# Fused RWKV attention and two MoE stages: filler transposes only in the first part, later expected landings, and a small expert slot whose first products keep the tokens stationary

## The chip, the cores and the metric

One core of a Trainium2 chip (trn2) runs the whole program in one launch. The metric is the device time of a run in microseconds (us); smaller is better. The engines are TensorE (PE; its weight loads are shown as PEld), VectorE (DVE), ScalarE (ACT), GpSimd (POOL) and SyncE (SP, which issues most DMAs). "PEq", "SPq" and so on are the engines' sequencers.

## What is computed

Three stages follow each other; 3072 tokens (4 sequences of 768), width 384.

```python
# 1. attention, 8 heads of 48, state S per head, in time order
y[t] = r[t] @ (S + outer(u * k[t], v[t]));  S = w * S + outer(k[t], v[t])
# 2. dense feed-forward layer, 384 -> 2048 -> 384
h = x @ w_in;  x2 = silu(h) @ w_out
# 3. top-1 mixture of 8 experts, 384 -> 1024 -> 384
logits = x2 @ w_gate + modality_bias[modality_id];  e = argmax(logits)
out = softmax(logits)[e] * (relu(x2 @ w1[e]) @ w2[e])
```

## The kernel before, in words

**Tiles.** Attention runs in chunks: 24 tiles of 128 tokens, tile n belonging to block j = n//3 of 384 tokens. `load_A` (L284, 768 KB, tile name in_av) and `load_B` (L287, 384 KB, in_rk) bring a tile's inputs into one of the buffers AB_132, AB_133 or `stall`. L460 (DVE) scales a tile by the decay table Pt, L464, L435 and L436 (POOL) do more of the scaling, L439 and L440 (DVE) a row sum, L487 and L503 (PE) are the products, L493 (DVE) masks them, L544 is the state's product. After the loads stands L425, a store that is taken only in a rare case, but whose place on SP waits for the landing of `load_A`.

**Dense layer.** `moe1` takes a block of 384 tokens through 16 chunks of the hidden width. Every 32-bit product is done as three products of high and low halves (hi by hi, hi by lo, lo by hi). L618 is a first product (9 matmuls, stationary 128x128, 384 columns moving), L622 and L623 the SiLU on ACT, L625 the low half on DVE, L637 the second products. L653 and L655 drain a block's result into x2all.

**Routing.** `route` transposes the block (L686, nine transposes), takes logits (L697) and a string of small DVE operations (L702 to L774), stores the tokens and their gate (`x_rows`, L764, three stores of 192.5 KB on SP) and scatters their numbers into the experts' lists (L780, POOL).

**Experts.** `expert(s)` is called for nine static slots, s = 0 to 8. Slots 0 to 7 hold 384 tokens each. Slot 8 is `small`: one tile of 128 tokens. First products are L949 (`e_g1`), relu and split are L1034 (ACT) and L1036 (DVE), second products L957 (`e_g2`), scaling by the gate L961 or L963, and the rows go out by an indirect DMA on POOL (L966). In the small slot there are two groups k of four chunks of the hidden width each: w1 stands as the stationary 128x128 operand and the 128 tokens move, so a group is 4 x 9 = 36 matmuls of 128 columns, and writes h transposed, as the second products need it. After the slots comes a loop for left-over tiles (L1077, L1078), which with these inputs runs no turn; the engines' sequencers meet at it.

**Order.** All of this up to the loop is not written in the order in which it runs. Every step is added to a `Plan` (class at L60, `add` at L65) with an engine, a duration, a priority, dependencies and buffers. `order()` (L74) plays it through when the program is built: a free engine takes the ready step with the lowest priority number; a DMA's data counts as landed 4.0 us after its share of one common transfer line. The steps are then issued sorted by planned start, so each engine has a fixed order and real waits are by semaphores. One hundred filler steps of four transposes of the identity each (L372, PE, priority 900 and up, called dummies below) take what PE time is left free in the plan.

Of the kernel before, what the change touches and what calls it, by code (L numbers as in the profile page):

```python
# [8 lines left out]
F32 = mybir.dt.float32  # L9
# [4 lines left out]
AF = mybir.ActivationFunctionType  # L14
ALU = mybir.AluOpType
AX = mybir.AxisListType
SP = mybir.EngineType.SP
# [9 lines left out]
KT = DM // 128  # L27
# [15 lines left out]
NZ = 9  # L43
# [13 lines left out]
class Plan:  # L57
# [7 lines left out]
    def add(self, eng, dur, prio, fn, deps=(), acq=(), rel=(), lat=0.2, nbytes=0):  # L65
        o = Op()
        o.eng, o.dur, o.prio, o.fn, o.lat, o.nbytes = eng, dur, prio, fn, lat, nbytes
        o.deps = [d for d in deps if d is not None]
        o.acq, o.rel = list(acq), list(rel)
        o.n, o.after, o.left = len(self.ops), [], 0  # L70
        self.ops.append(o)
        return o

    def order(self):  # L74
        for o in self.ops:
            o.left = len(o.deps)
            for d in o.deps:
                d.after.append(o)
        ready = {e: [] for e in ENGINES}
        busy = dict.fromkeys(ENGINES, 0.0)  # L80
        events, dma, t, done = [], 0.0, 0.0, []
        for o in self.ops:
            if not o.left:
                heapq.heappush(ready[o.eng], (o.prio, o.n, o))
        count = 0
        while True:
            moved = True
            while moved:
                moved = False
                for e in ENGINES:  # L90
                    if busy[e] > t + 1e-9 or not ready[e]:
                        continue
                    held, pick = [], None
                    while ready[e]:
                        x = heapq.heappop(ready[e])
                        need = {}
                        for p, _ in x[2].acq:
                            need[p] = need.get(p, 0) + 1
                        if all(len(self.free[p]) >= k for p, k in need.items()):
                            pick = x[2]  # L100
                            break
                        held.append(x)
                    for x in held:
                        heapq.heappush(ready[e], x)
                    if pick is None:
                        continue
                    o = pick
                    for p, key in o.acq:
                        self.slot[key] = (p, self.free[p].pop(0))
                    o.start = t  # L110
                    busy[e] = t + o.dur
                    end = t + o.dur + o.lat
                    if o.nbytes:
                        dma = max(dma, t + o.dur) + o.nbytes / 260e3
                        end = dma + 4.0
                    heapq.heappush(events, (busy[e], count, None))
                    heapq.heappush(events, (end, count + 1, o))
                    count += 2
                    done.append(o)
                    moved = True  # L120
            if not events:
                break
            t = events[0][0]
            while events and events[0][0] <= t + 1e-9:
                o = heapq.heappop(events)[2]
                if o is None:
                    continue
                for key in o.rel:
                    p, i = self.slot[key]
                    self.free[p].append(i)  # L130
                for a in o.after:
                    a.left -= 1
                    if not a.left:
                        heapq.heappush(ready[a.eng], (a.prio, a.n, a))
        assert len(done) == len(self.ops), (len(done), len(self.ops))
        self.span = t
        return sorted(done, key=lambda o: (o.start, o.n))


def moe_rwkv_kernel(tc, ins, out):  # L140
    nc = tc.nc
    vv, gp, act, pe, sp = nc.vector, nc.gpsimd, nc.scalar, nc.tensor, nc.sync
# [13 lines left out]
    hps = [ps.tile([128, 512], F32, name=f"ph{i}") for i in range(2)]  # L156
    aps = [ps.tile([128, 512], F32, name=f"pa{i}") for i in range(3)]
    tps = [ps.tile([128, 512], F32, name=f"pt{i}") for i in range(3)]
# [3 lines left out]
    ident = cst.tile([128, 128], F32, name="ident")  # L162
# [120 lines left out]
    def load_A(n, s):  # L283
        sp.dma_start(AB[s][:, 0:AW], ins["av"][n])  # L284

    def load_B(n, s, w_=0):
        sp.dma_start(AB[s][:, AW + w_ * DM:], ins["rk"][n * C:(n + 1) * C, w_ * DM:])  # L287
# [52 lines left out]
    for i in range(NP):  # L340
        n = 1 << i
# [12 lines left out]
    add = P.add  # L354
# [4 lines left out]
    def sl_(key):  # L359
        return P.slot[key][1]  # L360
# [47 lines left out]
    def attention(n):  # L408
# [5 lines left out]
        if n < 3:  # L414
            P.slot[kA] = ("tA", n)
            if n < 2:
                P.free["tA"].remove(n)
            oA, oB = gate((0.1, 0.2, 2.2)[n]), add("SP", 0.5, -49 + n, lambda: load_B(n, n, 1), nbytes=200e3)
        else:
            oA = add("SP", 0.6, z - 9, lambda: load_A(n, sl_(kA)), acq=[("tA", kA)], nbytes=786e3)  # L420
            oB = add("SP", 0.6, z - 8.9, lambda: load_B(n, sl_(kA), int(n < NZ)), [oA], nbytes=393e3 if n >= NZ else 197e3)
        relA = [kA] if n != 2 else []

        def f_V():
# [469 lines left out]
    def e_view(buf, p):  # L894
        t = W[p][buf].rearrange("p a b -> p (a b)")
        n = KT * FE
        return t[:, 0:n].rearrange("p (k f) -> p k f", k=KT), t[:, n:2 * n].rearrange("p (f d) -> p f d", f=NFE)
# [46 lines left out]
    def e_g1(buf, xb, fcs, n, p):  # L944
        w1h, w1l = e_view(buf, 0)[0], e_view(buf, 1)[0]
        for i, fc in enumerate(fcs):
            ops = [(kt, a, b_) for a, b_ in ((w1h, xh), (w1l, xh), (w1h, xl)) for kt in range(KT)]
            for m, (kt, a, b_) in enumerate(ops):
                pe.matmul(p[:, i * n:(i + 1) * n], a[:, kt, fc * 128:(fc + 1) * 128], b_[xb][:, kt, 0:n],  # L949
                          start=m == 0, stop=m == len(ops) - 1)  # L950

    def e_g2(buf, fcs, t, n, hi, lo, a):
        w2h, w2l = e_view(buf, 0)[1], e_view(buf, 1)[1]
        for i, fc in enumerate(fcs):
            sl = slice(i * n + t * 128, i * n + (t + 1) * 128)
            for m, (g, wt_) in enumerate(((hi, w2h), (hi, w2l), (lo, w2h))):
                pe.matmul(a[:, 0:DM], g[:, sl], wt_[:, fc, :], start=fc == 0 and m == 0, stop=fc == NFE - 1 and m == 2)  # L957
# [17 lines left out]
    def swap():  # L975
        at.release()
        ew = pools["ew"] = tc.alloc_tile_pool(name="ew", bufs=1)
        pools["raw"] = [ew.tile([128, KT * FE], F32, name=f"raw{i}") for i in range(4)]
        pools["xg"] = [ew.tile([128, XW], F32, name=f"xgb{i}") for i in range(2 * BT)]
        pools["gt"] = [[ew.tile([128, 1], F32, name=f"gt{i}{k}") for k in range(BT)] for i in range(NSTAT + 1)]  # L980

# [2 lines left out]
    def expert(s):  # L984
# [43 lines left out]
        for k, fcs in enumerate(groups):  # L1028
            kH, kG = ("eh", s, k), ("eg", s, k)
            m = n * step  # L1030
            o1 = add("PE", 2.7 if small else 1.57, z + k * (1.0 if small else 1.0), lambda fcs=fcs, kH=kH: e_g1(buf, xb, fcs, n, hps[sl_(kH)]),
                     [o_sp[0, p_] for p_ in range(3)] + o_x, acq=[("h", kH)])
            em["g1", s] = em["g1", s] + [o1]
            o2 = add("ACT", 0.62 if small else 0.5, z + k - 6, lambda kH=kH, kG=kG, m=m: act.activation(  # L1034
                ghb[sl_(kG)][:, 0:m], hps[sl_(kH)][:, 0:m], AF.Relu), [o1], acq=[("g", kG)])
            o3 = add("DVE", 0.7 if small else 0.57, z + k - 6, lambda kH=kH, kG=kG, m=m: vv.scalar_tensor_tensor(  # L1036
                glb[sl_(kG)][:, 0:m], hps[sl_(kH)][:, 0:m], 0.0, ghb[sl_(kG)][:, 0:m].bitcast(F32), op0=ALU.max, op1=ALU.subtract),
                [o2], rel=[kH])
            need = [o_sp[1, p_] for p_ in range(((0, 0, 0, 1, 1, 1, 2, 2)[fcs[-1]]) + 1)] + [o3, lastg]

            def f_g2(fcs=fcs, kG=kG):
                for t in range(nt_):
                    e_g2(buf, fcs, t, n, ghb[sl_(kG)], glb[sl_(kG)], aps[sl_(ka[t])])
            lastg = add("PE", 2.1 if small else 1.57, z + k + 2.3, f_g2, need, acq=[("a", q) for q in ka] if k == 0 else [], rel=[kG])
            em["g2", s] = em["g2", s] + [lastg]
# [27 lines left out]
        expert(s)  # L1073
    with tc.manual_schedule():
        for o in P.order():
            o.fn()
    tn = nc.values_load(tailn, min_val=0, max_val=NMAX - NSTAT + NA + 1)  # L1077
    with tc.For_i(0, tn, 1) as i:  # L1078
        e_ids("t", lists[1], bass.ds(i + (NSTAT - 1 - NA), 1))
# [91 lines left out]
```

## Time and profile before

| | us |
|---|---|
| median of three runs (lowest to highest) | 808.32 (807.42 to 811.14) |
| the profiled execution, its own time | 806.15 |
| its span in the trace | 804.4 |
| PE busy | 791.2 (98%) |
| DVE, ACT, POOL busy | 425.7, 337.3, 227.9 |
| mean granted TensorE clock | 0.995 |

The span runs from the first to the last instruction in the trace; the 1.75 us between it and the execution's own time lie outside. A busy share tells how full an engine is, not whether its work is of use: the dummies count as busy PE. The granted clock is the share of full TensorE speed that the chip allowed in a stretch; its two levels are 1.2 and 2.4 GHz, so 0.5 is the lower one.

### The profile page before, as it was taken

How to read it: one execution, taken by the hardware profiler on the slowest of the kernel's cores; microseconds unless marked ns; L12 is line 12 of the kernel's file. 1: busy time of each engine (PE TensorE's matmuls, PEld its weight loads, DVE VectorE, ACT ScalarE, POOL GpSimd, SP SyncE). 2: the span in 40 equal slices, each digit the busy share in tenths (PEclk: the TensorE clock that was granted, in tenths of full speed). 3: DMA queues.
4: the chain of work that ended last, by engine and by line, in shares of the span. 5: the costliest groups of instructions: out<-in, count | busy, mean ns of one | idle time of the engine just before them, and what ended most of it. 6: DMA issues, size and time to landing. Idle time of an engine off the chain costs nothing.

```text
span 804.4 us, 15749 instructions
## 1 busy us (share of the span) xinstructions
PE 791.2 (98%) x6348; PEld 760.0 (94%) x6348; DVE 425.7 (53%) x793; ACT 337.3 (42%) x726; POOL 227.9 (28%) x280
## 2 busy tenths in 40 slices
PE   8999999998999999999999999999999999999998
PEld 7998999987999999999999999999999999999998
DVE  7989965635534543644643522353866544654310
ACT  3566765443334334334334422364435434444200
POOL 5435302343423422522421203210432313220120
PEclk9999999998999999999999999999999999999999
DMA  6454433081511411411421024531675345500000
GB/s 245 153 177 184 167 119 108 28 79 44 90 59 59 91 60 60 89 60 61 85 65 59 11 22 180 224 120 68 217 217 187 128 135 199 196 28 1 30 35 2
DMA packets 23920, 83.27 MB, mean 104 GB/s; under 512 B 7659, under 2 KB 12152, under 8 KB 21538
## 3 DMA queue, kind: packets, MB, share of 16 engines
q1 hardware_dynamic: 19730, 72.55, 30.1%
q0 software_dynamic: 3968, 9.66, 3.6%
q8 instruction: 51, 0.84, 0.5%
q14 instruction: 27, 0.22, 0.2%
q10 hardware_dynamic: 144, 0.00, 0.0%
HBM read 78.92 MB, written 9.77 MB: 110 GB/s over the span
## 4 chain that ended last, share of the span: by engine, by line
PE 90%; DVE 4%; DMA 3%; issue 1%; ACT 1%; POOL 1%; DVEq 0%; POOLq 0%; SPq 0%; ACTq 0%
PE ph L618 24%; PE pa L637 23%; PE ph L949 13%; PE pa L957 12%; PE pt L503 4%; PE pa L372 3%; PE pt L487 3%; PE ph L372 2%; DMA xgb<-x_rows,it 2%; DMA AB<-in_av_dram 1%; PE pt L933 1%; PE ph L305 1%; PE pt L686 1%; PE pt L544 1%; PE pt L697 1%
## 5 line engine op out<-in xcount | busy, mean ns | idle before, releaser
L625 DVE TENSOR_TENSOR gl<-sg,gh 128x384 fp32r<-128x384 f32 x128 | 86.7, 677 | 136.4 <-ACT gh L623 135.9
L622 ACT ACTIVATE sg<-ph 128x384 f32<-128x384 f32 x128 | 63.0, 492 | 214.0 <-PE ph L618 205.6
L637 PE MATMUL pa<-Wh,gh 128*128 128x384 f32 x384 | 132.7, 346 | 0.0
L637 PE MATMUL pa<-Wh,gl 128*128 128x384 f32 x384 | 129.7, 338 | 0.5 <-DVE gl L625 0.4
L637 PE MATMUL pa<-Wl,gh 128*128 128x384 f32 x384 | 128.8, 335 | 0.0
L618 PE MATMUL ph<-xh,Wh 128*128 128x384 f32 x384 | 92.8, 349 | 0.0
L618 PE MATMUL ph<-xh,Wl 128*128 128x384 f32 x384 | 88.9, 339 | 0.1
L618 PE MATMUL ph<-xl,Wh 128*128 128x384 f32 x384 | 88.5, 338 | 0.0
L1034 ACT ACTIVATE gh<-ph 128x384 fp32r<-128x384 f32 (+1 forms) x66 | 32.7, 495 | 113.5 <-PE ph L949 112.9
L1036 DVE SCALAR_TENSOR_TENSOR gl<-ph,gh 128x384 fp32r<-128x384 f32 (+1 forms) x66 | 36.8, 558 | 81.1 <-ACT gh L1034 81.1
L637 PEld LDWEIGHTS pa<-Wh,gh 128*128 128x128 f32 x384 | 72.3, 188 | 3.2 <-issue 2.0
L637 PEld LDWEIGHTS pa<-Wh,gl 128*128 128x128 f32 x384 | 72.1, 188 | 1.2 <-DVE gl L625 1.2
L637 PEld LDWEIGHTS pa<-Wl,gh 128*128 128x128 f32 x384 | 72.3, 188 | 0.0
L618 PEld LDWEIGHTS ph<-xh,Wh 128*128 128x128 f32 x384 | 66.3, 189 | 4.8 <-issue 3.2
L966 POOL DMA_INDIRECT out_dram<-x2all,it x25 | 33.8, 1353 | 127.8 <-DVE x2all L963 114.6
L618 PEld LDWEIGHTS ph<-xh,Wl 128*128 128x128 f32 x384 | 69.3, 188 | 0.7 <-DVE Wl L596 0.7
L618 PEld LDWEIGHTS ph<-xl,Wh 128*128 128x128 f32 x384 | 69.5, 189 | 0.0
L929 DVE TENSOR_TENSOR Wl<-raw,Wh 128x1024 fp32r<-128x1024 f32 (+2 forms) x54 | 64.0, 1220 | 9.9 <-ACT Wh L925 9.9
L957 PE MATMUL pa<-Wh,gh 128*128 128x384 f32 x200 | 67.6, 338 | 0.8 <-DVE x2all L963 0.8
L957 PE MATMUL pa<-Wh,gl 128*128 128x384 f32 x200 | 67.5, 337 | 0.0
L957 PE MATMUL pa<-Wl,gh 128*128 128x384 f32 x200 | 67.0, 335 | 0.0
L475 ACT ACTIVATE atall<-ident,cs 128x128 f32<-128x128 f32 x176 | 57.2, 393 | 13.8 <-DVE cs L457 9.8
(226 smaller groups left out, 1385.2 us busy)
## 6 DMA issues: line engine op xcount, KB each, us to landing
raw<-in_we_dram SPq DMA_DIRECT2D x18, 1536.0 KB
AB<-in_av_dram SPq DMA_DIRECT2D x18, 768.0 KB
stall<-in_wio_dram SPq DMA_DIRECT2D x16, 768.0 KB
x_rows<-x2all SPq DMA_DIRECT2D x24, 192.5 KB
AB<-y_slow SPq DMA_DIRECT2D x16, 256.0 KB
stall<-in_av_dram SPq DMA_DIRECT2D x5, 768.0 KB
AB<-in_rk_dram SPq DMA_DIRECT2D x10, 384.0 KB
stall<-in_rk_dram SPq DMA_DIRECT2D x5, 384.0 KB
```

The lines of the kernel that those rows point to most:

```text
L372: add("PE", 0.45, 900 + i, lambda i=i: [pe.transpose(bank(("w", i))[:, 0:128], ident, ident) for _ in range(4)], acq=[("ha"[i % 2], ("w", ...
L475: act.activation(atb[sl_(kT)][h % 2][:, h // 2, :], ident, AF.Copy, scale=cs[:, h:h + 1])
L618: pe.matmul(p, win(a, fc, kt), (xh, xl)[b_][j % 2][:, kt, :], start=i == 0, stop=i == len(ops) - 1)
L622: o_s = add("ACT", 0.5, s - 4, lambda: act.activation(sgb[sl_(kS)], hps[sl_(kH)][:, 0:n], AF.Silu), [o_g1], acq=[("sg", kS)])
L625: o_l = add("DVE", 0.55, s - 4, lambda: vv.tensor_tensor(glb[sl_(kG)][:, 0:n], sgb[sl_(kS)], ghb[sl_(kG)][:, 0:n].bitcast(F32), op=ALU.sub ...
L637: pe.matmul(a, g[:, ts], wout(wp_, fc), start=begin and i == 0, stop=end and i == 2)
L929: eng.tensor_tensor(e_view(buf, 1)[wi][sl], m2[s]["raw", wi][sl], e_view(buf, 0)[wi][sl].bitcast(F32), op=ALU.subtract)
L949: pe.matmul(p[:, i * n:(i + 1) * n], a[:, kt, fc * 128:(fc + 1) * 128], b_[xb][:, kt, 0:n], start=m == 0, stop=m == len(ops) - 1)
L957: pe.matmul(a[:, 0:DM], g[:, sl], wt_[:, fc, :], start=fc == 0 and m == 0, stop=fc == NFE - 1 and m == 2)
L966: i = gp.indirect_dma_start(out=out, out_offset=bass.IndirectOffsetOnAxis(ap=m2[s]["it"][:, t:t + 1], axis=0), in_=o, in_offset=None, boun ...
L1034: o2 = add("ACT", 0.62 if small else 0.5, z + k - 6, lambda kH=kH, kG=kG, m=m: act.activation(ghb[sl_(kG)][:, 0:m], hps[sl_(kH)][:, 0:m], ...
L1036: o3 = add("DVE", 0.7 if small else 0.57, z + k - 6, lambda kH=kH, kG=kG, m=m: vv.scalar_tensor_tensor(glb[sl_(kG)][:, 0:m], hps[sl_(kH)][ ...
```

## The change

1. When the sorted steps are issued, dummies whose planned start is 150 us or later are left out.
2. In the plan a DMA's data now counts as landed 3.8 us plus the step's own `lat` after its transfer; the default of 0.2 gives the 4.0 of before. For the tiles from n = 9 on (NZ is 9), `load_A` gets 8.0 (11.8 in all) and `load_B` 6.0 (9.8 in all). No instruction is added or taken away by this: only the order in which the engines take their steps moves.
3. In the small slot the two halves of the tokens (xh, xl) are the stationary operand and w1 moves, 512 columns wide: 9 matmuls a group. The result has tokens in partitions, so ACT takes the relu into a new tile `hn`, PE turns it by four transposes into a PSUM tile (`e_tn`), ACT copies that to the high half and DVE subtracts for the low half. The second products are as before.

```diff
@@ order()
-                        end = dma + 4.0
+                        end = dma + 3.8 + o.lat
@@ attention(n)
-            oA = add("SP", 0.6, z - 9, lambda: load_A(n, sl_(kA)), acq=[("tA", kA)], nbytes=786e3)
-            oB = add("SP", 0.6, z - 8.9, lambda: load_B(n, sl_(kA), int(n < NZ)), [oA], nbytes=393e3 if n >= NZ else 197e3)
+            oA = add("SP", 0.6, z - 9, lambda: load_A(n, sl_(kA)), acq=[("tA", kA)], nbytes=786e3, lat=8.0 if n >= NZ else 0.2)
+            oB = add("SP", 0.6, z - 8.9, lambda: load_B(n, sl_(kA), int(n < NZ)), [oA], nbytes=393e3 if n >= NZ else 197e3, lat=6.0 if n >= NZ else 0.2)
@@ new functions
+    def e_g1n(buf, xb, k, p):
+        w1h, w1l = e_view(buf, 0)[0], e_view(buf, 1)[0]
+        ops = [(kt, a, b_) for b_, a in ((xh, w1h), (xh, w1l), (xl, w1h)) for kt in range(KT)]
+        for m, (kt, a, b_) in enumerate(ops):
+            pe.matmul(p, b_[xb][:, kt, 0:128], a[:, kt, k * 512:(k + 1) * 512], start=m == 0, stop=m == len(ops) - 1)
+
+    def e_tn(g, p):
+        for i in range(4):
+            pe.transpose(p[:, i * 128:(i + 1) * 128], g[:, i * 128:(i + 1) * 128], ident)
@@ expert(s), small slot only (the others keep their three steps)
+        pools["hn"] = [ew.tile([128, 512], F32, name=f"hn{i}") for i in range(1)]
...
+                o1 = add("PE", 2.1, z + k, lambda k=k, kH=kH: e_g1n(buf, xb, k, hps[sl_(kH)]), [o_sp[0, p_] for p_ in range(3)] + o_x,
+                         acq=[("h", kH)])
+                o2 = add("ACT", 0.62, z + k - 6, lambda kH=kH: act.activation(
+                    pools["hn"][0], hps[sl_(kH)], AF.Relu), [o1], rel=[kH])
+                o2 = add("PE", 0.45, z + k - 6, lambda kN=kN: e_tn(pools["hn"][0], tps[sl_(kN)]), [o2], acq=[("t", kN)])
+                o2 = add("ACT", 0.62, z + k - 6, lambda kG=kG, kN=kN: act.activation(ghb[sl_(kG)], tps[sl_(kN)], AF.Copy), [o2],
+                         acq=[("g", kG)])
+                o3 = add("DVE", 0.7, z + k - 6, lambda kG=kG, kN=kN: vv.tensor_tensor(
+                    glb[sl_(kG)], tps[sl_(kN)], ghb[sl_(kG)].bitcast(F32), op=ALU.subtract), [o2], rel=[kN])
@@ issue of the sorted steps
-            o.fn()
+            if o.prio < 900 or o.start < 150.0:
+                o.fn()
```

What the diff does not show is where the order moves. On DVE, around the end of block 1 in the dense layer (L653 drains it; AB_132 holds tile 10 and AB_133 tile 11), before:

```order
L625 TENSOR_TENSOR gl_126<-sg_119,gh_123 128x384
L460 TENSOR_TENSOR AB_133<-AB_133,Pt 128x512
L653 TENSOR_TENSOR x2all<-pa_80,x2all 128x384
L653 TENSOR_TENSOR x2all<-pa_79,x2all 128x384
L653 TENSOR_TENSOR x2all<-pa_81,x2all 128x384
L625 TENSOR_TENSOR gl_124<-sg_120,gh_121 128x384
```

and with the change:

```order
L653 TENSOR_TENSOR x2all<-pa_80,x2all 128x384
L653 TENSOR_TENSOR x2all<-pa_79,x2all 128x384
L653 TENSOR_TENSOR x2all<-pa_81,x2all 128x384
L625 TENSOR_TENSOR gl_125<-sg_119,gh_122 128x384
L625 TENSOR_TENSOR gl_126<-sg_120,gh_123 128x384
L493 COPY_PREDICATED atall<-mask,pt_84 128x512
L493 COPY_PREDICATED atall<-mask,pt_83 128x512
L460 TENSOR_TENSOR AB_133<-AB_133,Pt 128x512
```

L460 of tile 11 stood directly ahead of the drain; it now stands seven instructions behind the drain's start, after the masks of tile 9. On SP, the same stretch, before:

```order
L284 DMA AB_132<-in_av_dram 128x1536
L287 DMA AB_132<-in_rk_dram 128x768
L425 ISA
L425 DMA AB_132<-y_slow 128x512
L764 DMA x_rows<-x2all 128x385 x3
L284 DMA AB_133<-in_av_dram 128x1536
L287 DMA AB_133<-in_rk_dram 128x768
```

and with the change, up to the loads of the tile after (n = 12, in `stall`), which take the same form:

```order
L284 DMA AB_132<-in_av_dram 128x1536
L764 DMA x_rows<-x2all 128x385 x3
L284 DMA AB_133<-in_av_dram 128x1536
L287 DMA AB_132<-in_rk_dram 128x768
L425 ISA
L425 DMA AB_132<-y_slow 128x512
L287 DMA AB_133<-in_rk_dram 128x768
L425 ISA
L425 DMA AB_133<-y_slow 128x512
L284 DMA stall<-in_av_dram 128x1536
L764 DMA x_rows<-x2all 128x385 x3
L287 DMA stall<-in_rk_dram 128x768
```

The three stores of block 1 are ahead of tile 11's loads in both orders; now they are ahead of tile 10's second load too, which also stands behind tile 11's first load. The stores of block 2 come between tile 12's two loads now, and the same holds for tiles 15, 18 and 21. On PE, the last slot from its first group on, before (one of its groups k, and the dummies behind it):

```order
L949 MATMUL ph_78<-xl_117,Wh_73 128x128 x3
L957 MATMUL pa_79<-Wh_74,gh_123 128x384
...
L957 MATMUL pa_81<-Wh_74,gl_126 128x384
L372 MATMUL ph_77<-ident 128x128 x4
L372 MATMUL ph_78<-ident 128x128 x4
L372 MATMUL ph_77<-ident 128x128 x4
L957 MATMUL pa_80<-Wh_73,gh_121 128x384
```

and with the change:

```order
L960 MATMUL pt_83<-ident,hn_5312 128x128 x4
L956 MATMUL ph_78<-Wh_73,xh_115 128x512 x3
L956 MATMUL ph_78<-Wl_75,xh_115 128x512 x3
L956 MATMUL ph_78<-Wh_73,xl_117 128x512 x3
L967 MATMUL pa_79<-Wh_74,gh_123 128x384
...
L967 MATMUL pa_81<-Wh_74,gl_126 128x384
L960 MATMUL pt_82<-ident,hn_5312 128x128 x4
L967 MATMUL pa_80<-Wh_73,gh_121 128x384
```

Each group of 36 matmuls became 9 wide ones, its four transposes stand behind the nine second products that follow (of slot 7's last two chunks), and the dummies are gone: three steps (twelve transposes) here, one between the slot's two groups of second products, and 51 behind its last product, 220 transposes in all. Ahead of this slot PE's order is the same step by step.

## Rows read from the trace of the kernel before

**Rows 1.** What PE waited for (total us, times, longest us), whole span.

```profile
PE pt L686 <- DVE x2all L653: 4.4, 1, 4.4
```

**Rows 2.** Chain that ended last, 760 to 805 us: start, duration, what.

```profile
761.80 3.97 PE ph L949 x36
765.76 1.61 PE pa L957 x9
...
772.96 1.31 PE ph L372 x12
774.27 2.09 PE pa L957 x12
776.36 0.44 PE pa L372 x4
...
778.89 8.30 PE pa L372 x76
```

**Rows 3.** Timeline, last DVE and POOL steps: start, duration, idle before and releaser.

```profile
778.93 0.62 DVE L963 TENSOR_SCALAR x2all<-pa,gt 128x384 f32<-128x384 f32 x1 [5.17 <-PE pa L957]
779.82 0.98 POOL L966 DMA_INDIRECT out_dram<-x2all,it  x1 [2.69 <-DVEq L1078]
```

**Rows 4.** SP's waits, 770 to 805 us.

```profile
SPq L1078 <- PEq L1077: 16.8, 1, 16.8
```

**Rows 5.** Sequencer instructions of line L1078: count, ns min/median/max, first and last start.

```profile
L1078 ACTq EVENT_SEMAPHORE  x13: 17/38/16749, 773.1 to 799.7; - x13
...
L1078 PEldq EVENT_SEMAPHORE  x13: 51/51/51, 801.2 to 803.0; - x13
```

**Rows 6.** Timeline 764 to 768 us: the small slot's relu and split.

```profile
765.80 0.60 ACT L1034 ACTIVATE gh<-ph 128x512 fp32r<-128x512 f32 x1 [5.03 <-PE ph L949]
766.43 0.69 DVE L1036 SCALAR_TENSOR_TENSOR gl<-ph,gh 128x512 fp32r<-128x512 f32 x1 [5.08 <-ACT gh L1034]
```

**Rows 7.** Chain that ended last, 170 to 190 us.

```profile
172.33 1.59 PE ph L618 x9
...
173.97 9.30 DMA AB<-in_av_dram
...
184.63 1.54 PE pt L686 x6
186.18 2.88 PE ph L618 x9
189.06 0.63 PE pt L686 x3
```

**Rows 8.** DVE's timeline in the same stretch.

```profile
183.29 0.69 DVE L460 TENSOR_TENSOR AB<-AB,Pt 128x512 f32<-128x512 f32 x1 [6.72 <-DMA AB<-in_av_dram]
184.02 1.49 DVE L653 TENSOR_TENSOR x2all<-pa,x2all 128x384 f32<-128x384 f32 x3
```

**Rows 9.** Windows: length, busy time of PE, PEld, DVE, ACT, POOL, granted clock, DMA share, GB/s.

```profile
180.00:185.00 5.00, 0.56 (x4) 0.37 (x3) 1.67 (x4) 0.49 (x1) 1.66 (x1) 0.77 0.44 175
185.00:190.00 5.00, 5.00 (x21) 4.90 (x20) 2.77 (x4) 2.02 (x5) 3.55 (x4) 0.55 0.00 2
780.00:804.40 24.40, 21.16 (x194) 20.92 (x192) 0.00 (x0) 0.00 (x0) 0.88 (x2) 0.99 0.02 5
```

**Rows 10.** Chain, 140 to 150 us: the nine transposes of the block before.

```profile
142.90 0.33 PE pt L686 x3
...
144.79 0.66 PE pt L686 x6
```

**Rows 11.** SP's timeline, 155 to 226 us.

```profile
163.12 1.29 SPq L764 DMA_DIRECT2D x_rows<-x2all  x3
...
200.50 0.33 SPq L284 DMA_DIRECT2D stall<-in_av_dram  x1
...
204.95 0.09 SPq L425 DMA_DIRECT2D stall<-y_slow  x1
```

**Rows 12.** DVE's timeline, 203 to 228 us: tile 12's row sum.

```profile
214.66 0.56 DVE L439 TENSOR_REDUCE cs<-stall 128x8 f32<-128x384 f32 x1
```

More of the change, by code (lines that the diff above doesn't have):

```diff
@@ L1030, in expert @@
             m = n * step
[L1031 to L1038, printed above, removed]
+            if small:
+                kN = ("en", s, k)
+                o1 = add("PE", 2.1, z + k, lambda k=k, kH=kH: e_g1n(buf, xb, k, hps[sl_(kH)]), [o_sp[0, p_] for p_ in range(3)] + o_x,
[7 more added lines that the diff above has]
+                    glb[sl_(kG)], tps[sl_(kN)], ghb[sl_(kG)].bitcast(F32), op=ALU.subtract), [o2], rel=[kN])
+            else:
+                o1 = add("PE", 1.57, z + k * 1.0, lambda fcs=fcs, kH=kH: e_g1(buf, xb, fcs, n, hps[sl_(kH)]),
+                         [o_sp[0, p_] for p_ in range(3)] + o_x, acq=[("h", kH)])
+                em["g1", s] = em["g1", s] + [o1]
+                o2 = add("ACT", 0.5, z + k - 6, lambda kH=kH, kG=kG, m=m: act.activation(
+                    ghb[sl_(kG)][:, 0:m], hps[sl_(kH)][:, 0:m], AF.Relu), [o1], acq=[("g", kG)])
+                o3 = add("DVE", 0.57, z + k - 6, lambda kH=kH, kG=kG, m=m: vv.scalar_tensor_tensor(
+                    glb[sl_(kG)][:, 0:m], hps[sl_(kH)][:, 0:m], 0.0, ghb[sl_(kG)][:, 0:m].bitcast(F32), op0=ALU.max, op1=ALU.subtract),
+                    [o2], rel=[kH])
```

## The prediction

> **What bounds the kernel now.** I read the page's busy shares first: PE is busy 98% of the span, so outside PE only the ends and PE's waits can hold time, and inside PE the question is which of its work is of use. PE's waits come next: a single one stands behind the first part, 4.4 us until DVE's L653 [rows 1]. Then the chain at the end: the last product begins its group at 776.79 (2.09 us) and is followed at 778.89 by dummies alone [rows 2]. 204 of them at 8.30/76 = 0.109 us make 22.3 us, up to 801.2, where PE's sequencer gets on with the loop's branch [rows 5]. Meanwhile the last result is scaled at 778.93 and sent at 779.82 [rows 3], and SP, which waits for that landing, then waits 16.8 us more for PE's sequencer [rows 4]; ACT is let go at 799.7 [rows 5]. So the kernel ends with filler that everybody waits for. The windows show PE at a granted clock of 0.99 there, against 0.77 and 0.55 at 180 to 190 us [rows 9].
>
> **The change part by part.** The sum is made against the profiled execution, 806.15 us; the median of the runs, 808.32, is 2.2 us above it.
>
> *(a) Dummies behind the last product, -18.1.* Without them PE's sequencer is at L1077 long before the last landing, so the landing ends the wait: 799.6 - 16.8 = 782.8 [rows 4]. From there to the span's end lies at least what follows PE's drain now, 804.4 - 801.2 = 3.2 us, and at most what follows the release, 804.4 - 799.7 = 4.7 us [rows 5]. I take 3.5, since the branches that wait for PE's drain are part of the 4.7: the end is 786.3, 18.1 earlier (16.9 to 18.4). The chain L963, L966, landing itself is unchanged and was beside the dummies; now it is bare. The dummies of the first part stay, so nothing changes there.
>
> *(b) The small slot, -4.7.* Now, from 761.80 to 778.89, two groups of 36 matmuls (3.97 each), the nine second products of slot 7 twice (1.61 and 1.62), twelve dummies (1.31), four dummies (0.44) and twice twelve second products (2.09 each), together 17.1 us [rows 2]. After it, a group is 9 matmuls of 512 columns. No row has 512. By columns from 384 (1.61/9 = 0.179 each; at full pace 1.58/9 = 0.175, as L618's 1.59 shows [rows 7]) it is 0.233, so 2.10 a group; on the line through 128 columns (3.97/36 = 0.110) and 384 it is 0.208, so 1.87. I take 2.10, since from 384 up a matmul has been paced by its columns, not its load; 1.87 stays as the low end, and as high end 0.110 for a load that is not hidden on top, 3.1 a group. To that come 2 x 0.44 for four transposes, priced as four dummies [rows 2]. Sum after: 2 x 2.10 + 1.61 + 1.62 + 2 x 0.44 + 2 x 2.09 = 12.5, a gain of 4.6; with the small pieces of pace 4.7 (2.7 to 5.1).
>
> The Trainium skill (TensorE: Matmul & The Clock Gate, "Back-to-back issue gap") gives a sustained spacing of about 131 ns for 512 columns. By it the two groups would be 2.4 us and not 4.2, and the sum 1.8 us lower; the trace's 0.175 us for only 384 columns is already above it, so the measurement decides.
>
> Does PE wait in the new chain? The relu (0.60 [rows 6]) lies beside nine second products (1.61) that stand between a group and its transposes: 1.0 spare. Behind the transposes the copy and the subtract cost about 0.60 + 0.69 plus hand-overs, 1.4 in all; for the first group 3.7 us of PE work cover them, for the second the 2.09 us of the first group's second products: 0.7 spare. Those write pa_80, which slot 7's scaling has to free: its last three products end 0.54 (a third of 1.61) before slot 7 does, the scaling takes about 0.62 [rows 3], and the 0.44 of transposes cover the rest. Without cover, each costs some tenths of a us at most. The extra ACT and POOL work is none elsewhere.
>
> *(c) The landings, -6.9.* At 173.97 SP issues tile 11's load behind the three stores of 163.12, and it lands 9.30 later [rows 7, 11]; tile 12's at 200.50, with no stores ahead, takes 4.45 until SP goes on at 204.95 [rows 11]. DVE waits 6.72 us in L460 for it, with the drain L653 queued behind [rows 8], and PE waits 4.4 us for the drain [rows 1]. With the change the drain is ahead of L460, so this wait has no reason left. After it PE ran at 0.55 [rows 9]: a group of L618 took 2.88 against 1.59, 1.29 lost, and nine transposes 1.54 + 0.63 = 2.17 against 0.99 in the block before [rows 7, 10], 1.18 lost. Together 4.4 + 2.5 = 6.9 us (0 to 6.9).
>
> The moved steps cost nothing by these rows. Stores and loads have the same bytes and the same number of issues. L460 of tile 11 now waits where the low halves of its neighbours have been done, and the tile's products come two blocks of work later. Tile 10's second load now stands behind tile 11's first: at the 9.30 of [rows 7] it lands near 184 and its row sum slips from 175 to about 189, still ahead of its products on PE. Tile 12's second load stands behind block 2's stores. L439 of that tile runs at 214.66 now [rows 12]; issued at 202 to 206 and landing 4.5 to 9.3 later it is there at 207 to 215. If that cover goes, DVE is held, with the low halves L625 that PE needs queued behind it.
>
> Sum: 18.1 + 4.7 + 6.9 = 29.7; 806.15 - 29.7 = 776.5 in an execution like the profiled one, 778.6 from the median. I forecast 778.0.
>
> **The rivals.** (1) *The stall stays or comes back elsewhere.* SP's queue is as full as before around 174 us, and a wait on a load could move to L439 of tile 10 or into POOL's scaling. For: tile 10's second load is later than it was. Against: the drain stands ahead of all of them now. One stall of this kind is 6.9: 784.9.
>
> (2) *The clock falls at the end.* Without dummies the small slot has no filler. For: the clock fell at the one place where PE stood still [rows 9]. Against: by (b) no wait of that length arises. All of the slot at 0.55 would cost 12.5 x (1/0.55 - 1) = 10.2: 788.
>
> (3) *Slower: the second loads come late.* From tile 10 on, at five places (tiles 10, 12, 15, 18 and 21), they queue behind stores that wait for the routing's gates on DVE. If the load lands after DVE comes to L439, DVE stands, PE waits for L625, and the clock falls as at 180 us: 6.9 a place, 34.5 at five, so 778 + 34.5 = 812.5. It decides at a landing at 214.66 for tile 12 [rows 12], and the late end above, 215, is only just there; but a hold of 0.5 us on DVE does not stop PE, and all five would have to go wrong.
>
> (4) *Wide matmuls as fast as the cited spacing:* 776.2. (5) That the change does not do what it says is excluded: the order shows the dummies gone and L460 moved.
>
> **How the numbers follow.** The forecast has 0.76, rival 1 0.15, rival 2 0.03, rival 3 0.03, rival 4 0.03. The forecast's own range is 774.5 (the profiled execution's sum, with the low end of (b) and a little pace) to 782. To leave out no more than 2 in 10 the range goes on through rival 1 (784.9, plus the spread of 2.6 us that the runs of before show above the profile): 774.5 to 787.5. A measurement can tell about 0.5%, 4.0 us: below 804.3 is faster. Only rival 3, or two others together, reaches there, and half of its 0.03 stays within the bound: faster 0.97, same 0.015, slower 0.015.
>
> **What would show it.** PE's last product is followed by no L372, and SP's wait of 16.8 us for PE's sequencer is gone. The nine wide matmuls of a group take 2.1 us, and PE has no wait at the transposes' heirs. L653 of block 1 starts at about 177, and the windows from 180 to 190 show a clock of 0.99 or more. I am wrong if PE waits anew for L625 or L653, if the clock falls in a window before 765 us, or if more than 5 us lie between the last landing and the end.

## The result

The changed kernel takes 781.97 us (median of four runs, 780.03 to 783.16) against 809.73 us (807.42 to 813.01) for the kernel before: a ratio of 0.965, 95% interval 0.961 to 0.969. The forecast was 778.0 in 774.5 to 787.5. The profiled execution of the change took 782.15 us, its span is 780.4 us; the working of the forecast, made against the profiled execution of before, had come to 776.5.

The page of the changed kernel, part 1, and then what PE waited for (columns as in [rows 1]):

```profile
PE 763.5 (98%) x6082; PEld 731.3 (94%) x6082; DVE 405.4 (52%) x793; ACT 338.5 (43%) x728; POOL 221.0 (28%) x280
```

```profile
PE pt L503 <- issue: 3.3, 1, 3.3
PE pa L330 <- DVE neq L329: 3.2, 1, 3.2
PE pt L487 <- POOL AB L464: 1.1, 1, 1.1
PE pa L967 <- issue: 0.8, 1, 0.8
PE ph L618 <- issue: 0.6, 1, 0.6
```

The wait of 4.4 us for L653 [rows 1] is gone. In its place stand two waits on "issue", for which the profile shows no releaser: 3.3 us in L503 and 0.6 us in L618. Such a wait is called a hole below. (The third, 0.8 us in L967 at 586 us, is not new: the trace of before has the same 0.8 us there, behind L963.)

**The end.** The last steps on DVE and POOL, then ACT's sequencer at the loop (count, ns min/median/max, first and last start), then SP's waits from 730 us on:

```profile
773.28 0.62 DVE L973 TENSOR_SCALAR x2all<-pa,gt 128x384 f32<-128x384 f32 x1 [2.85 <-PE pa L967]
...
774.18 0.98 POOL L976 DMA_INDIRECT out_dram<-x2all,it  x1 [2.02 <-DVEq L1102]
```

```profile
L1102 ACTq EVENT_SEMAPHORE  x13: 17/38/1002, 769.7 to 777.2; - x13
```

```profile
SPq L1190 <- PEq L1190: 3.0, 2, 2.4
```

PE's last product ends at 773.25, the span at 780.4: 7.2 us, where it was 804.4 - 778.9 = 25.5 us. The longest wait on ACT's sequencer fell from 16.7 us [rows 5] to 1.0.

**The small slot.** PE's timeline:

```profile
760.78 0.85 PE L956 MATMUL ph<-Wh,xh 128*128 128x512 f32 x3
761.47 0.85 PE L956 MATMUL ph<-Wl,xh 128*128 128x512 f32 x3
762.15 0.85 PE L956 MATMUL ph<-Wh,xl 128*128 128x512 f32 x3
762.84 0.34 PE L967 MATMUL pa<-Wh,gh 128*128 128x384 f32 x1
...
764.40 0.60 PE L960 MATMUL pt<-ident,hn 128*128 128x128 f32 x4
764.76 0.95 PE L956 MATMUL ph<-Wh,xh 128*128 128x512 f32 x3
```

A group takes 762.84 - 760.78 = 2.06 us for nine matmuls, 0.229 each; no row has an idle time before it. From the first wide matmul to the last product it is 773.25 - 760.78 = 12.5 us, against 17.1 [rows 2].

**The stall.** Windows at 180 us (columns as in [rows 9]) and DVE's timeline:

```profile
180.00:185.00 5.00, 5.00 (x33) 4.96 (x32) 3.51 (x7) 2.51 (x6) 0.00 (x0) 1.00 0.64 191
185.00:190.00 5.00, 5.00 (x54) 4.40 (x53) 2.35 (x4) 1.64 (x4) 3.70 (x4) 1.00 0.27 109
```

```profile
179.86 0.69 DVE L460 TENSOR_TENSOR AB<-AB,Pt 128x512 f32<-128x512 f32 x1
180.46 1.05 DVE L625 TENSOR_TENSOR gl<-sg,gh 128x384 fp32r<-128x384 f32 x2
181.54 1.49 DVE L653 TENSOR_TENSOR x2all<-pa,x2all 128x384 f32<-128x384 f32 x3
```

PE is busy throughout at a granted clock of 1.00. The drain starts at 181.54 where the prediction said about 177: PE's last product of the block ended at 178.6 already in the trace of before, and this execution had lost 2 us by then (see the end). (The stores at 163 us and the drain at 184 us in [rows 8, 11] belong to blocks 0 and 1: the block numbers given ahead with the SP order are one too high for the stores.)

**The holes.** PE's timeline at the longer one, then POOL's before it:

```profile
403.75 0.86 PE L503 MATMUL pt<-AB,S 128*32 128x128 f32 x24
404.43 1.04 PE L503 MATMUL pt<-atall,AB 128*32 128x128 f32 x27
408.79 0.43 PE L503 MATMUL pt<-atall,AB 128*32 128x128 f32 x5 [3.32 <-issue]
```

```profile
391.01 1.20 POOL L780 DMA_INDIRECT id_list<-ids_c,r_si  x1 [0.81 <-DVE r_si L774]
...
392.52 0.97 POOL L780 DMA_INDIRECT id_list<-ids_c,r_si  x1 [0.21 <-issue]
...
393.79 0.98 POOL L780 DMA_INDIRECT id_list<-ids_c,r_si  x1 [0.22 <-issue]
```

PE stops inside one run of 32 equal matmuls, whose operands were all there for the 27 before. The DMA view of 400 to 411 us has a single packet, on the queue that brings PE's instructions (it has 51 packets in the trace of before, 49 in the change's with 220 dummies less, 47 in run 6's with no dummy):

```profile
q8 instruction: 1, 0.02, 1.8%
```

That is 16 KB, and 1.8% of 16 engines' 11 us is 3.2 us. It starts at 400.7 and has landed at 403.9, 1.6 us before the hole begins. Between 140 and 560 us of six traces (before, changed, and the first four runs below) such a packet takes 1.07 us in the median (108 packets, at most 1.47) when the last of the scatters L780 began 16 us or more before, but 2.78 us (33 packets, 28 of them over 1.6) when it began 3 to 10 us before. This gave the theory that the experiments then tried.

### The profile page after: what moved, and what is told of

The parts are those of the page before. It is cut to its first block, busy times and chain, and to the rows that moved or that the text cites. A ratio compares the mean times of both kernels' runs of the same rounds, so it can differ in the third digit from the quotient of the medians.

```text
span 780.4 us, 15228 instructions
## 1 busy us (share of the span) xinstructions
PE 763.5 (98%) x6082; PEld 731.3 (94%) x6082; DVE 405.4 (52%) x793; ACT 338.5 (43%) x728; POOL 221.0 (28%) x280
## 5 line engine op out<-in xcount | busy, mean ns | idle before, releaser
L622 ACT ACTIVATE sg<-ph 128x384 f32<-128x384 f32 x128 | 62.9, 491 | 216.4 <-PE ph L618 191.5
L625 DVE TENSOR_TENSOR gl<-sg,gh 128x384 fp32r<-128x384 f32 x128 | 80.5, 629 | 143.7 <-ACT gh L623 132.7
L618 PE MATMUL ph<-xh,Wh 128*128 128x384 f32 x384 | 92.5, 348 | 0.6 <-issue 0.6
L618 PE MATMUL ph<-xh,Wl 128*128 128x384 f32 x384 | 88.9, 339 | 0.0
L618 PE MATMUL ph<-xl,Wh 128*128 128x384 f32 x384 | 88.5, 338 | 0.0
L1057 ACT ACTIVATE gh<-ph 128x384 fp32r<-128x384 f32 x64 | 31.4, 490 | 103.5 <-PE ph L949 92.7
L618 PEld LDWEIGHTS ph<-xh,Wh 128*128 128x128 f32 x384 | 65.9, 188 | 5.7 <-issue 4.1
L1059 DVE SCALAR_TENSOR_TENSOR gl<-ph,gh 128x384 fp32r<-128x384 f32 x64 | 35.5, 554 | 68.7 <-ACT gh L1057 68.6
L618 PEld LDWEIGHTS ph<-xh,Wl 128*128 128x128 f32 x384 | 69.1, 188 | 0.5 <-DVE Wl L596 0.5
L618 PEld LDWEIGHTS ph<-xl,Wh 128*128 128x128 f32 x384 | 69.5, 189 | 0.0
L967 PE MATMUL pa<-Wh,gh 128*128 128x384 f32 x200 | 67.4, 337 | 0.8 <-issue 0.8
L967 PE MATMUL pa<-Wh,gl 128*128 128x384 f32 x200 | 67.4, 337 | 0.0
L967 PE MATMUL pa<-Wl,gh 128*128 128x384 f32 x200 | 67.0, 335 | 0.0
```

The source lines that it names most:

```text
L618: pe.matmul(p, win(a, fc, kt), (xh, xl)[b_][j % 2][:, kt, :], start=i == 0, stop=i == len(ops) - 1)
L622: o_s = add("ACT", 0.5, s - 4, lambda: act.activation(sgb[sl_(kS)], hps[sl_(kH)][:, 0:n], AF.Silu), [o_g1], acq=[("sg", kS)])
L625: o_l = add("DVE", 0.55, s - 4, lambda: vv.tensor_tensor(glb[sl_(kG)][:, 0:n], sgb[sl_(kS)], ghb[sl_(kG)][:, 0:n].bitcast(F32), op=ALU.sub ...
L1057: o2 = add("ACT", 0.5, z + k - 6, lambda kH=kH, kG=kG, m=m: act.activation(ghb[sl_(kG)][:, 0:m], hps[sl_(kH)][:, 0:m], AF.Relu), [o1], acq ...
L1059: o3 = add("DVE", 0.57, z + k - 6, lambda kH=kH, kG=kG, m=m: vv.scalar_tensor_tensor(glb[sl_(kG)][:, 0:m], hps[sl_(kH)][:, 0:m], 0.0, ghb[ ...
```

## The experiments

Twelve runs; the first four, the next four, the next three and the last stood on chips of their own, so each is compared with the runs of before beside it. "Holes" are the waits of PE on "issue" before 575 us in that run's trace.

| run | median us (before beside it) | ratio, 95% interval | span | holes us |
|---|---|---|---|---|
| profiled before | 809.73 | | 804.4 | 0 |
| the change | 781.97 (809.73) | 0.965, 0.961 to 0.969 | 780.4 | 3.9 |
| 1 the change again | 783.96 (808.97) | 0.970, 0.965 to 0.976 | 778.3 | 3.2 |
| 2 dummies alone | 790.61 (808.97) | 0.977, 0.972 to 0.983 | 789.0 | 3.6 |
| 3 landings alone | 805.61 (808.97) | 0.997, 0.994 to 1.000 | 802.5 | 2.3 |
| 4 slot alone | 808.06 (808.97) | 1.001, 0.997 to 1.004 | 803.1 | 1.4 |
| 5 without the landings | 784.35 (807.29) | 0.971, 0.964 to 0.978 | 781.3 | 2.6 |
| 6 no dummies | 779.33 (807.29) | 0.964, 0.955 to 0.973 | 778.3 | 1.4 |
| 7 scatters later | 782.73 (807.29) | 0.967, 0.960 to 0.975 | 782.5 | 5.3 |
| 8 scatters twice | 855.14 (807.29) | 1.058, 1.048 to 1.069 | 851.3 | 54.4 |
| 9 scatters spread | 774.95 (804.72) | 0.963, 0.960 to 0.967 | 772.7 | 0 |
| 10 spread, no dummies | 777.07 (804.72) | 0.964, 0.961 to 0.968 | 775.6 | 0 |
| 11 no dummies again | 778.45 (804.72) | 0.966, 0.963 to 0.970 | 776.4 | 0.6 |
| 12 spread, without the landings | 780.70 (809.09) | 0.964, 0.960 to 0.968 | 780.1 | 0 |

**1. The change again** (no edit).

> The changed kernel once more, for what repeats. Theory A (chance): the hole of 3.3 us on PE at 405 us and the 2 us lost before 60 us belong to that one execution; this trace has neither at these places, and its span is 775 to 778. Theory B (the new order): the hole stands at the same place, among tile 21's products of L503, and the span is 780 again.

Neither theory as it stood. The hole at 405 us and the 2 us before 60 us are not there (the same SiLU step L622 starts at 59 us in the changed kernel's first trace and 3.6 us earlier in this one), but the span is 778.3, since there are other holes: 2.1 and 0.5 us at 174 to 177, 0.6 at 343.

```profile
PE ph L618 <- issue: 2.6, 2, 2.1
```

The first stands where the change's hole of 0.6 us in L618 stood. Counted in PE's matmuls, whose order is the same up to the last slot, all 14 holes of the change and of runs 1 to 5 and 7 lie at four places: 1603 to 1613, 1947 to 1953, 3130 to 3131 and 3691 to 3694. So the places recur, and which of them are taken, and for how long, changes from one execution to the next. Each of these holes, and the two of runs 6 and 11, begins 9.7 to 13.7 us after the last scatter of a block has begun.

**2. Dummies alone.** Before, with the issue of steps limited:

```diff
-            o.fn()
+            if o.prio < 900 or o.start < 150.0:
+                o.fn()
```

> The kernel before with the late dummies left out and nothing else. My step (a): 18.4 us behind the last product, and 1.75 us more for the 16 transposes inside the small slot, if PE does not wait there instead: 788 to 790 against 809. Rival (the dummies hold the clock up): the granted clock falls in the small slot, and the gain is under 12 us. The stall of 4.4 us at 180 us stays.

The span falls by 804.4 - 789.0 = 15.4 us, but this trace has 3.6 us of holes and a stall of 5.0, where the profiled execution of before had none and 4.4. PE's waits:

```profile
PE pt L686 <- DVE x2all L653: 5.0, 1, 5.0
...
PE pt L544 <- issue: 1.9, 1, 1.9
PE pt L503 <- issue: 1.1, 1, 1.1
```

Counted from the same step of slot 7 at 760 us, which is 4.0 us later here, the end comes 19.4 us sooner; expected were 18.4 + 1.75 = 20.1. The median, 790.61, is just above the expected 788 to 790. The granted clock is 1.00 in each 5 us from 760 to 780: no loss there.

**3. Landings alone.** Before, with the two `lat` values and `end = dma + 3.8 + o.lat`.

> The kernel before with the later landings in the plan alone. My step (c): the stall at 180 us is gone, with the slower clock after it: -6 to -7 us, 802 to 803 against 809. Rival (the new order has a wait of its own): a hole of 3 us or more among L503 or L487 of a tile from 12 on, and a gain of 2 to 3 us only.

Median -3.4 us, between the two; the ratio's interval allows a gain of 0 to 5 us, less than the 6 to 7 expected. The stall is gone, and holes are there:

```profile
PE ph L618 <- issue: 1.2, 1, 1.2
PE pt L503 <- issue: 1.1, 1, 1.1
```

This trace is also 3.6 us behind the one of before at 57 us, where no engine's order had changed; between the two steps L622 that stand at 156 and 198 us in before's trace it takes 37.1 us, where before took 42.5.

**4. Slot alone.** Before, with the new slot and all dummies.

> The kernel before with the turned small slot alone; all 100 dummies stay. The two groups 2 x (3.97 - 2.1) less 2 x 0.44 for the transposes: -2.9 us, since the dummies that no longer fit into the slot run behind it. Rival (wide matmuls pay their load, or PE waits at the transposes): -0.5 to +1 us.

The time doesn't move, yet PE finishes earlier: its last dummy ends at 796.7 instead of 801.2, 4.5 us sooner, of which 1.4 were there before the slot, so 3.1 for it. They are lost after PE's end. SP's waits:

```profile
SPq L1189 <- PEq L1189: 5.9, 2, 5.4
```

Here the engines meet PE's sequencer once more behind the loop, and that wait is 5.4 us, 2.4 in the changed kernel (above). What makes it longer wasn't tried.

**5. Without the landings.** The changed kernel with `end = dma + 4.0` and without the two `lat` values.

> The changed kernel with the landings as before: what part 2 is worth beside the other two. My step (c): 6.9 us slower than the changed kernel (782 to 784), so 789 to 791, with PE's wait of 4.4 to 5 us at 180 us back and the slower clock after it. Rival (most of it is given back by holes on PE that hang on the new order): 785 to 787, the same wait, and no hole over 0.5 us at 174 to 178 and 405 us.

The stall is back, with holes at other places than the changed kernel's, and the median is 2.4 us above 781.97, on another chip; by the ratios to before (0.971 and 0.965, whose intervals overlap) it is about 5 us. So the time doesn't decide between the two. The rival's reason is not borne out, since holes belong to either order.

```profile
PE pt L686 <- DVE x2all L653: 3.6, 1, 3.6
...
PE pt L544 <- issue: 2.0, 1, 2.0
...
PE pt L503 <- issue: 0.6, 1, 0.6
```

**6. No dummies.** The changed kernel with `if o.prio < 900:`.

> The changed kernel without any dummy, so also without the 180 transposes of the first part. Theory A (they fill time that PE has to wait anyway): the time is the same, 782 to 784, and PE's waits grow by some 19 us before 135 us, at a clock of 0.98 or more. Theory B (they hold the clock up): the granted clock falls to 0.8 or less somewhere before 135 us, and the time is 790 or more.

Neither. The clock does fall, and it costs nothing that this run can show (run 10 comes back to it). Windows:

```profile
0.00:25.00 25.00, 18.32 (x187) 16.89 (x187) 21.19 (x51) 9.08 (x17) 15.11 (x33) 0.84 0.66 229
25.00:50.00 25.00, 20.28 (x181) 17.95 (x181) 23.69 (x25) 15.53 (x32) 13.22 (x9) 0.89 0.49 175
50.00:75.00 25.00, 21.71 (x210) 18.23 (x211) 20.43 (x27) 15.40 (x33) 6.87 (x5) 0.80 0.47 166
```

PE also waits 1.3 us for the drain L653 at 181 us here, behind a step L622 that ACT took only at 179.8 us, 4.5 us after its last; why is not shown.

**7. Scatters later.** The changed kernel; behind the call that adds L780, and where the steps are sorted:

```diff
+            routed["id", j, t].late = j not in (1, 3, NB - 1)
-        for o in P.order():
+        for o in sorted(P.order(), key=lambda o: o.start + 8.0 * getattr(o, "late", False)):
```

> The changed kernel with the scatters of blocks 0, 2, 4, 5 and 6 issued 8 us later in the plan on POOL, all other engines' orders the same. Theory F (the scatters delay PE's instruction fetches, and a late fetch leaves a hole on PE): the fetches near 173 and 401 us, which took 2.9 to 3.3 us in all three traces with the new order, take about 1 us, the holes at 178 and 405 us are gone, and slow fetches stand again only 3 to 10 us behind a scatter. Theory C (chance, or another transfer): the fetches near 173 and 401 us stay at 3 us although no scatter stands ahead of them. In time at most 1 to 3 us less, which the runs can hardly tell.

Inconclusive: POOL takes a step as soon as it is next and its data is there, so in block 4 the scatters ran at 389.8 to 392.4 us as ever, and only block 0's moved (168.6 instead of 163.9). The packet at 398 us took 3.5 us, and the hole after it, which begins 1.1 us behind its landing, is the longest but for run 8's:

```profile
PE pt L503 <- issue: 5.3, 1, 5.3
```

**8. Scatters twice.** The changed kernel; `id_s2` and `idl2` are a second group and table:

```diff
+                apart(id_s2, gp.indirect_dma_start(
+                    out=idl2, out_offset=bass.IndirectOffsetOnAxis(ap=T_["si"][:, t], axis=0), in_=ids_c[:, n:n + 1],
+                    in_offset=None, bounds_check=NE * SLOT - 1, oob_is_err=False))
```

> The changed kernel with each scatter followed by a second one of the same numbers into another table that nobody reads. Theory F: twice the scatters keep PE's fetches slow for longer: fetches up to 16 us behind the last of them take 2 us or more (in the traces so far 2 of 12 did between 10 and 16 us), the holes on PE grow to 6 us or more in sum, and the time is 2 to 6 us longer. Theory C: fetches and holes as in the changed kernel; POOL is some 9 us busier and PE doesn't show it.

855.14 us, 73 more than the change. Of the 70.9 us that the span grew, PE's waits on "issue" are 54.4:

```profile
PE pt L504 <- issue: 31.4, 13, 9.6
PE pa L638 <- issue: 15.7, 6, 7.8
PE pt L545 <- issue: 7.3, 1, 7.3
```

Twenty-four more scatters of 128 rows, behind which nobody waits, stop PE for up to 9.6 us at a time (lines are one higher here). Theory C falls, and F had the size wrong by over ten. The packets themselves didn't become longer than 3.3 us but for one of 8.6, so the packet's duration isn't the measure of the delay. Nor is a packet under way in most of the holes: of the 16 holes of the change and of runs 1 to 7 and 11, 9 begin after the packet before them has landed, 5 while one is under way, and 2 with none in the 9 us before. So that scatters bring PE's holes about is shown; that they do it by holding up these packets is not.

**9. Scatters spread.** Run 7's sorting, with

```diff
+            routed["id", j, t].late = 10.0 + 20.0 * t if j < 5 else 0.0
-        for o in P.order():
+        for o in sorted(P.order(), key=lambda o: o.start + getattr(o, "late", 0.0)):
```

> The changed kernel with the three scatters of each of blocks 0 to 4 taken apart on POOL: the first 10, the second 30 and the third 50 us later in its planned order, so that a tile's work stands between two of them; the other engines' orders are the same. Theory F (a burst of scatters delays PE's instruction fetches): fetches over 2 us before 420 us are 0 or 1 (4 in the changed kernel's trace), PE has no hole without a releaser over 0.6 us before 450 us, and the time is 1 to 4 us less than the changed kernel's 782 to 784. Theory C (the holes have another cause): holes of 1 to 5 us near 178, 216, 345 or 405 us as before.

PE's waits in full, and POOL's timeline at block 4:

```profile
PE pa L330 <- DVE neq L329: 3.2, 1, 3.2
PE pa L968 <- issue: 0.8, 1, 0.8
PE pa L637 <- DVE gl L625: 0.4, 1, 0.4
```

```profile
389.08 1.03 POOL L780 DMA_INDIRECT id_list<-ids_c,r_si  x1 [0.15 <-issue]
...
404.45 1.01 POOL L780 DMA_INDIRECT id_list<-ids_c,r_si  x1 [0.15 <-issue]
...
429.00 1.26 POOL L780 DMA_INDIRECT id_list<-ids_c,r_si  x1 [0.15 <-issue]
```

Now the scatters are 15 and 25 us apart, and no hole is left before 575 us. The expectation on the packets missed: five still take 2.5 to 3.5 us before 420. A single scatter slows a packet too, and PE stands still behind none in this run or in runs 10 and 12; three in a row can make it stop (block 5's three, at 444.8 to 447.4 us, stayed together here and did not). Three traces with spread scatters have no hole; of the ten with bursts of three, nine have some, and only the profiled execution of before has none. The median is 774.95, ratio 0.963; on its chip before was 804.72, so the 7 us to the change's median are partly the chip's, and the ratios overlap. The spans are 772.7 here, 780.4 and 778.3 for the change.

**10 and 11. Without dummies,** with the scatters spread and as they were.

> Spread scatters and no dummy at all. If the two are independent: the gain of the spread kernel plus the 0 to 3 us that the kernel without dummies showed, 776 to 780. If the slower clock before 75 us costs anything, it is no faster than the spread kernel.

> The changed kernel without any dummy again, timed in more rounds. Theory A: the dummies of the first part change nothing, 781 to 784. Theory D (they delay PE's own work, a step that becomes ready waits behind a dummy): 1 to 3 us less, 779 to 781, with the first chunks of the dense layer up to 1.5 us earlier.

On one chip: spread 774.95, spread without dummies 777.07, without dummies alone 778.45. The dummies of the first part are worth nothing or 2 us: run 10's trace is 2.0 us behind run 9's at the same step L622 at 140 us, and the runs' times overlap. Leaving them out is no gain, and the theory that they delay PE's own work has no support. Of all kernels run, 9 has the lowest time; its ratio is not clear of the others'.

**12. Spread, without the landings.** Run 9's edit on run 5's kernel.

> The spread kernel with the landings as before: step (c) alone, measured where no hole disturbs it. My step (c): PE's wait at 180 us of 4 to 5 us and the slower clock behind it are back, and the span is 5.5 to 7 us above the spread kernel's 772.7: 778 to 780, a ratio to before near 0.970 against 0.963. Rival (the later landings gained little of their own): a span of 773 to 775, with a wait under 2 us at 180 us.

No hole in either trace, so step (c) can be read alone. Windows of this run, and PE's wait:

```profile
180.00:185.00 5.00, 1.49 (x7) 1.49 (x8) 2.79 (x5) 0.88 (x3) 2.74 (x2) 0.71 0.40 161
185.00:190.00 5.00, 5.00 (x21) 4.90 (x20) 1.65 (x2) 1.69 (x4) 2.48 (x2) 0.61 0.01 2
```

```profile
PE pt L686 <- DVE x2all L653: 3.7, 1, 3.7
```

The same L622 step starts 0.2 us later than in run 9 at 173 us and 6.7 us later at 191; the spans differ by 7.4. ACT's timeline in run 9 and then in this run:

```profile
173.34 0.49 ACT L622 ACTIVATE sg<-ph 128x384 f32<-128x384 f32 x1 [1.52 <-PE ph L618]
...
190.93 0.49 ACT L622 ACTIVATE sg<-ph 128x384 f32<-128x384 f32 x1
```

```profile
173.56 0.49 ACT L622 ACTIVATE sg<-ph 128x384 f32<-128x384 f32 x1 [2.96 <-PE ph L618]
...
197.61 0.49 ACT L622 ACTIVATE sg<-ph 128x384 f32<-128x384 f32 x1 [0.43 <-PE ph L618]
```

The times don't show it: the ratios to before, 0.964 and 0.963, differ by 0.6 us, and before itself differs by 4.4 us between the two chips.

## Why the prediction was right, and what it missed

The prediction held: faster, inside the range, 4 us above its number. Between the medians the gain is 27.8 us (809.73 - 781.97), and 25.0 on run 1's chip, of the 29.7 summed. Most of it is part (a), which run 2 shows by itself in the time, -18.4 us; the other two parts are shown in the traces, while the times of runs 3 and 4, which have one of them each, are not clear of no gain at all.

- **(a) Dummies, -18.1.** From the last product to the span's end 25.5 us became 7.2: -18.3. The rest after the last landing (774.18 + 2.6 = 776.8, with the 2.6 us that such a transfer took in the median in before's trace) is 3.6 us, 3.5 was taken.
- **(b) The small slot, -4.7.** 17.1 became 12.5: -4.6. A group is 2.06 us against 2.10, so 512 columns cost in proportion to 384, and PE doesn't wait at the transposes. The Trainium skill's sustained spacing of about 131 ns at 512 columns (TensorE: Matmul & The Clock Gate, "Back-to-back issue gap") is not what these rows show: 229 ns.
- **(c) The landings, -6.9.** At its place the stall was worth what was said: 6.7 us later at 191 us in run 12 than in run 9. From the step L622 at 156 us to the one at 191 to 198, the two traces of the old order without a hole take 42.5 and 42.0 us (before, run 12), the two of the new order 35.7 each (runs 9 and 10). Of its two halves the clock's is shown by the window at 0.61. That the kernel's time gains as much is not shown: run 3 gained 2 us by its ratio, at most 5.
- **What missed** is the basis of the sum: it took PE's idle time from one execution, and that execution had no hole at all. Of the three other traces of the old order with bursts (runs 2, 4 and 5) each has 1.4 to 3.6 us of them, and the five of the new order (the change, runs 1, 3, 6 and 7; run 11 has 0.6) 1.4 to 5.3. In the change's profile 3.9 us of holes and 2.0 us lost before 60 us, where no engine's order had changed, make 5.9; the miss against 776.5 was 782.15 - 776.5 = 5.7. So step (c) was right on the stall, and part of what it freed was taken by waits that before's trace had not shown. Whether the moved steps cost nothing, as the prediction has it, stays open: that the new order draws more holes than the old is not shown, since their number and sizes change between executions. What made the early 2 us isn't shown either; the same step L622 starts at 55 to 60 us in the traces of kernels that are alike up to there.
- **Signs.** Two of the signs that were named did not come as written. The drain started at 181.54 and not at 177 (at 177.9 in run 9, which has no hole). And the clock did fall in windows before 765 us, to 0.98 from 25 to 50 us and 0.96 from 50 to 75, in the part that the change doesn't touch. The others held.
- **Rivals.** The first (785, the stall comes back elsewhere) is the nearest to what came: time did come back elsewhere, but not from a load, and not by 6.9. The clock kept to 1.00 from 735 to 760 us and in each 5 us from 760 to 775, and fell to 0.89 only in a window that takes in the end without work. The second loads held up no product: PE has no wait on L625 beyond the 0.4 us that it had before, though DVE now stands in L439 until POOL has done its scaling, which it did not before:

```profile
DVE cs L439 <- POOL AB L436: 9.5, 4, 2.4
```

The spread of 2.6 us with which the range was carried through rival 1 has no source in the runs of before: their median lay 2.2 us and their highest 5.0 us above the profiled execution.

## What to carry to other kernels

Before a sum is made from one trace, look for what that trace lacks: the medians of before stood 2.2 and 3.6 us above the profiled execution (808.32 and 809.73 against 806.15), and other traces of the same order held 1.4 to 3.6 us of a wait that it had none of. A PE wait whose releaser is "issue" in the middle of equal matmuls comes from no engine that the profile can name; here it followed bursts of tiny indirect writes on another engine that PE doesn't wait for, and no trace had it once they were moved apart in that engine's order. Filler behind PE's own last work cost 18 us here, since every engine met PE's sequencer at the loop.

## What the runs showed of the hardware that was not expected

- **Scatters and PE.** Behind bursts of three indirect DMAs of 128 rows within 4 us PE stood still for up to 5.3 us, behind six within 8 us for up to 9.6; with the scatters taken apart over a block's time it did not, in three traces. PE's 16 KB instruction packets that start 3 to 10 us behind a scatter take 2.78 us in the median and not 1.07, yet 11 of the 16 holes of runs with bursts of three begin with no such packet under way. The Trainium skill (Runtime: NRT & Kernel Launch, "Instruction fetch mechanics") has the fetch in 16 KiB blocks, with which the packets agree, and calls its cost mostly hidden; whether the holes are part of that cost is not shown. Through what the scatters and PE meet is not shown.
- **Idle PE and the clock.** Waits of 4.4 and 3.7 us at 180 us were followed by 0.55 and 0.61 in the next window, while the hole of 3.3 us at 405 us left 1.00 in its own window and the next; run 7's of 5.3 us, at nearly the same place, was followed by 0.77 and 0.89.
- **A slower clock at little price.** In run 6 the clock was 0.80 to 0.89 up to 75 us, and the kernel was not measurably slower; PE was busy for only 18.3 to 21.7 us of each 25 there. Run 10 against run 9 leaves room for 2 us.
